# Gated attention unit and token mixer: keys turned as 64 rows, sums over tokens as 64x64 matmuls into one bank

## The chip, the core and the metric

The kernel runs on one core of a Trainium2 chip. The core has a matrix engine (TensorE, PE in the profile, with its weight loads as PEld), three engines for elementwise work (VectorE = DVE, ScalarE = ACT, GpSimd = POOL), a queue that issues DMAs (SyncE = SP) and 16 DMA engines. Matmuls read SBUF and write PSUM, which has eight banks of 2 KB for each of its 128 partitions; DVE and ACT take results out of PSUM, POOL does not read it. The metric is the device time of one execution in microseconds.

## What is computed

Eight sequences (b) of 3200 tokens, 256 wide. The first half is an attention without softmax, the second a token mixer on its result x.

```python
scores = (1.0 / S) * np.matmul(z, z.transpose(0, 2, 1))     # z: 8 x 3200 x 64
attn = np.maximum(scores, 0.0) ** 2
x = u * np.matmul(attn, v)                                   # u, v: 8 x 3200 x 256
wq, wk = x @ w_q, x @ w_k                                    # 256 -> 64
W_tok = (1.0 / 8.0) * np.einsum('bsd,btd->bst', wq, wk)
mixed = np.einsum('bst,btd->bsd', W_tok, x)
out = np.maximum(mixed, 0.0) @ w_out
```

No nonlinearity stands between W_tok and x, so the kernel never forms W_tok: it sums wk^T x over the tokens of a sequence, a 64 x 256 matrix, and multiplies wq by it. This sum over tokens is what the change is about.

## The kernel before

A sequence is cut into 25 tiles of 128 tokens and, for the columns of the attention, into seven groups: six of 512 tokens and a last one of 128 (LASTG). The stages of a sequence:

- Scores (L265). Two tiles of 128 x 512 scores go to one PSUM tile "ps" of two banks. There are two such tiles; scores, projections, mixes and output projections share them, so each new user waits until the one before the last has been read out. DVE or ACT applies ReLU (L291, L287) into g, and POOL or ACT squares it (L309, L307) into a buffer "at", of which there are NAT.
- Turned squares (L331). The attention matrix is symmetric, so blocks near the diagonal are computed once and turned by a DMA on SP into "tt" or "ttl".
- Second product (L352). Squares times v into "acc". Contraction over 128 tokens is split into two matmuls of 64 rows each, which write two banks (r = 0 and 1). A group's output has two halves, so four banks hold it.
- Gate. For each half of a group the two banks are added: one engine copies the first bank to SBUF (L368), DVE adds the second (L369), POOL multiplies by u into x (L388). x is stored so that one DMA (L400) turns it into xT.
- Projections (L417). x times w_q and w_k together, again as two 64-row halves. For half r = 0 of a group wqk holds [q, k] in its 128 columns and for r = 1 [k, q]; so queries of half r lie in partitions r * 64 onward, and keys in the other half of the partitions. Results are copied to "qk" (L430).
- Keys. One DMA (L435) turns all 128 rows of qk, queries included, into "kx", where each token has 64 places of queries and 64 of keys. POOL then writes the keys over the queries (doubling, L447), so that each token has its keys twice.
- Sums over tokens, "heads" in the code (L454). For each 128 tokens, two matmuls of 64 tokens each, with the doubled keys as 128 columns, into two banks: columns 256 to 511 of the PSUM tile whose first columns hold the next group's projections, or a tile of their own ("hd"). DVE adds both banks to "ha" (L469), and at the end of a sequence POOL adds the two halves into "hs" (L476). Because the keys were doubled, hs has the sum in both halves of its partitions, as the mixes need it.
- Mixes (L482) with ReLU out (L503), output projection (L513) with scaling out (L535, L540), store (L541).

The order of instructions on each engine is written out when the program is built. A planner keeps one clock for each engine, adds an assumed duration for each piece of work (give), and puts matmuls one after another; the extras (keys, mixes, projections) become ready at times in those clocks. `lead` sets how far scores run ahead of the second product; a pair p of score tiles may also be made only when the squares of pair p - NAT have been used. `shut` is the time at which the next bank of sums closes, and LATE, SPARE, BIAS shift choices between engines around it. MIXES spaces a sequence's mixes, V0 sets when the first loads of the second sequence's v begin, and KEEP how many tiles a group holds back for its end. DMAs on SP are entered by `move` with their issue time and the time they take on the DMA engines. The last sequence ends by code of its own (from L1082): x^T x for its last three groups ("xtx"), the remaining sum ("hd"), a product with w_k in fp32 ("hl", L565), then mixes and output projections without other work beside them.

Of the kernel before, what the change touches and what calls it, by code (L numbers as in the profile page):

```python
# [16 lines left out]
def kernel(  # L17
# [33 lines left out]

    NAT = 16
    NX = 7
    NXT = 4
    NEARBY = 8
    KEEP = 4

# [239 lines left out]
    def second_stage(p, g, ways):  # L297
        at = pat.tile([P, 2 * W], FP16, tag="at", name="at")
        at0 = 0
        parts = pieces(p)  # L300
        if len(ways) > len(parts):
            parts = [(slice(h, h + 1), parts[0][1]) for h in range(2)]
        for (hs, w), on_act in zip(parts, ways * 2):
            n = hs.stop - hs.start
            out = at[:, at0 : at0 + n * w].rearrange("p (n w) -> p n w", w=w)
            if on_act:
                nc.scalar.square(out=out, in_=g[:, hs, 0:w])  # L307
            else:
                nc.gpsimd.tensor_mul(out=out, in0=g[:, hs, 0:w], in1=g[:, hs, 0:w])  # L309
# [12 lines left out]
        def turn(b, gi, gj, n0, nn, c0, c1):  # L322
            if (b, gi, gj) not in turned:
                if gj == LASTG:
                    tag, nr, bufs = "ttl", 1, 8
                else:
                    homes[b, gi, gj] = home = homes_free.pop(0)
                    tag, nr, bufs = f"tt{home}", 4, 1
                turned[b, gi, gj] = ptt.tile([P, nr, 4, P], FP16, tag=tag, name=tag, bufs=bufs)
            out = turned[b, gi, gj][:].rearrange("p n j t -> p (n j) t")  # L330
            nc.sync.dma_start_transpose(out=out[:, 4 * n0 : 4 * (n0 + nn), :], in_=at[:, c0:c1])  # L331

        return [(x, lambda x=x: turn(*x)) for x in blocks]
# [27 lines left out]

    def gate(b, gi, half):
        if (b, gi) not in xs:
# [48 lines left out]

    def projections(b, gi, ps, stop=True):
        n = min(2, widths[gi] // P)
        for c in range(NC):
            for r in halves(gi):
                nc.tensor.matmul(  # L417
                    out=ps[:, r, 0 : n * P],
                    lhsT=wqk[top(r), c, :, :].rearrange("p t h -> p (t h)"),
                    rhs=xTs[b, gi][top(r), 0:n, c, :],  # L420
                    start=(c == 0),
                    stop=(stop and c == NC - 1),
                )

    def projections_out(b, gi, ps):
# [4 lines left out]
        nc.scalar.copy(out=qks[b, gi][:, 0:nr, 0 : n * P], in_=ps[:, 0:nr, 0 : n * P])  # L430

    def turn_keys(b, gi):
        nn = widths[gi] // P
        ks[b, gi] = pk.tile([P, 4, 2, dh], FP16, tag="kx", name="kx")
        nc.sync.dma_start_transpose(  # L435
            out=ks[b, gi][:, 0:nn, :, :].rearrange("p n a h -> p n (a h)"),
            in_=qks[b, gi][:].rearrange("p r s -> p (r s)")[:, 0 : nn * P],
        )

    doubled = set()  # L440

    def double_keys(b, gi):
        doubled.add((b, gi))
        nn = widths[gi] // P
        for r in halves(gi):
            sl = slice(2 * r, min(2 * r + 2, nn))
            nc.gpsimd.tensor_copy(out=ks[b, gi][:, sl, r, :], in_=ks[b, gi][:, sl, 1 - r, :])  # L447

    def heads(b, gi, ps, begun=()):
        nn = widths[gi] // P  # L450
        assert (b, gi) in doubled
        for n in range(nn):
            for r in range(2):
                nc.tensor.matmul(  # L454
                    out=ps[:, r, D : 2 * D],
                    lhsT=ks[b, gi][top(r), n, :, :].rearrange("p a h -> p (a h)"),
                    rhs=x_rows(b, gi, n)[top(r), :, :],
                    start=(n == 0 and r not in begun),
                    stop=(n == nn - 1),
                )  # L460
        del xs[b, gi]

    def heads_out(b, gi, ps):
        part = ps[:, 0:2, D : 2 * D]
        if gi == 0:
            hacc[b] = psml.tile([P, 2, D], FP32, tag="ha", name="ha")
            nc.vector.tensor_copy(out=hacc[b][:], in_=part)
        else:
            nc.vector.tensor_add(out=hacc[b][:], in0=part, in1=hacc[b][:])  # L469
        if gi == LASTG:  # L470
            heads_done(b)

    def heads_done(b):
        hss[b] = psml.tile([P, D], FP16, tag="hs", name="hs")
        ha = hacc.pop(b)
        nc.gpsimd.tensor_add(out=hss[b][:], in0=ha[:, 0, :], in1=ha[:, 1, :])  # L476

# [11 lines left out]

    def mix_out(b, gi, ps):  # L490
        n = min(2, widths[gi] // P)
# [10 lines left out]
        else:  # L502
            nc.scalar.activation(out=out, in_=ps[:, 0:nr, 0 : ND * n * P], func=RELU)  # L503

# [83 lines left out]
    mixed_at = []  # L588
    MIXES = 18.0
    MIXES_END = 14.0  # L590
# [82 lines left out]
    def squares():  # L673
        while pending and pending[0][0] <= clock[PE] + 0.3:
            ready, p, g = pending.pop(0)
            a, c = max(clock[ACT], ready), max(clock[POOL], ready)
            on_act = a + SPARE < c and (a + 1.06 <= shut() + LATE or a + 2.5 < c)
            ways = [on_act]
            if clock[PE] < UNTIL and max(a + 0.57, c + 0.97) + SPLIT < min(a + 1.06, c + 1.9):
                ways = [a < c, a >= c]  # L680
                done = max(give(ACT, ready, 0.57), give(POOL, ready, 0.97))
            else:
                done = give(ACT, ready, 1.06) if on_act else give(POOL, ready, 1.9)
            for (b, gi, gj, _, nn, _, _), turn in second_stage(p, g, ways):
# [20 lines left out]

    def double(b, gi):
        keys_at[b, gi] = give(POOL, clock[PE], 0.6) + 0.5
        double_keys(b, gi)

    def use_keys(b, gi):  # L710
# [3 lines left out]
        if keyed and keys_at.get(keyed[0], 1e9) <= clock[PE]:  # L714
            prior = keyed.pop(0)
        projections(b, gi, ps, stop=not prior)
        clock[PE] += 0.44 if gi < LASTG else 0.24
        if prior:
            heads(*prior, ps, halves(gi))
            clock[PE] += 0.44 if prior[1] < LASTG else 0.11  # L720
        ready = clock[PE] + FROM_PE
        projections_out(b, gi, ps)
        done = give(ACT, ready, 0.56)
        n = widths[gi] / P
        final = (b, gi) == (last, LASTG - 2)
        if not final:
            move(
                done + SLACK, done + 10.0, 1.28, 0.21 * n, lambda: turn_keys(b, gi),
                lambda t: at_time(t, lambda: double(b, gi)),
            )  # L730
            keyed.append((b, gi))
        if prior:
            heads_out(*prior, ps)
            done = give(DVE, done, 0.7)
            if prior[1] == LASTG:
                give(POOL, done, 0.6)
                heads_known(prior[0])
# [7 lines left out]
    def use_heads():  # L745
# [5 lines left out]
        heads_out(*prior, ps)  # L751
        done = give(DVE, clock[PE] + FROM_PE, 0.7)
        if prior[1] == LASTG:
            give(POOL, done, 0.6)
            heads_known(prior[0])
# [8 lines left out]
    def use_mix(b, gi):  # L764
# [3 lines left out]
        clock[PE] += 0.22  # L768
        mix_out(b, gi, ps)
        done = give(ACT, clock[PE] + FROM_PE, 1.03 if gi < LASTG else 0.3)  # L770
        close_slot(done)
# [40 lines left out]
    ZWAIT, ZDUE, ZSTEP, ZSTEP0 = 14.0, 32.0, 7.0, 5.0  # L812
    V0 = 56
    V1 = 11
# [37 lines left out]

    SPARE = 0.3
    BIAS = 0.2
    XDUE = 5.0
    XWAIT = 7.0
    LATE = 0.3

    def half_done(b, gi, half):
        ready = clock[PE] + FROM_PE  # L860
        t = give(ACT, ready, 0.57)
        t = give(DVE, t, 0.68)
        free_at[half] = t
        if b == last and gi >= LASTG - 2:
            give(DVE, t, 0.75)
        t = give(POOL, t, 1.2)
        gate(b, gi, half)
        if half == halves(gi)[-1]:
# [129 lines left out]
    done_acc = 0  # L998
    lead = 140
    turn_about = False  # L1000
# [40 lines left out]
    while extras or later or moves:  # L1041
        x = next((x for x in extras if x[1] == "proj"), None)
        if not x:
# [4 lines left out]
                or (x[1] == "keys" and len(keyed) < 2)  # L1048
                or keyed[0] in doubled
            ]  # L1050
# [39 lines left out]
    ha = hacc.pop(last)  # L1090
    nc.vector.tensor_add(out=hsum[:], in0=ha[:, 0, :], in1=ha[:, 1, :])
    psl = acc_tile(0, 1, "hl")
# [53 lines left out]
```

## Time and profile before

| | |
|---|---|
| median of 3 runs | 781.1 us (779.43 to 781.89) |
| the profiled execution | 780.0 us from first to last instruction |
| TensorE's granted clock, mean | 0.998 |
| DMA packets | 307116, 141.11 MB |
| DMA queue of SP: share of 16 engines | 85.8% |
| DMA queue of POOL: share of 16 engines | 14.6% |

The profile is of one execution. Busy time of TensorE counts each matmul from its start to a modelled end, so that two matmuls that overlap count once, and a short gap between starts can be covered by a modelled end. In groups of instructions a line reads: source line, engine, operation, tiles written and read, shapes, count, busy time, mean duration of one in ns, and idle time of the engine just before, with what ended it. In the timeline a row begins with its start and its duration, and the idle time before it stands in brackets.

### The profile page before, as it was taken

The page shows a single profiled execution, that of the slowest core. Times are in us where ns is not written, and L with a number is a line of the kernel's source. Part 1 is how long each engine was busy: PE and PEld are TensorE (multiplying, and loading weights), DVE is VectorE, ACT ScalarE, POOL GpSimd, SP SyncE. Part 2 cuts the span into 40 slices and gives each one's busy share as a digit, 9 for nine tenths or more (in the row PEclk, how much of TensorE's full clock was granted, in tenths as well). Part 3 has the DMA queues.
Part 4 walks back from the last instruction along what each step waited for, and adds up shares of the span by engine and source line. Part 5 has one row for each costly group of instructions (what it writes and reads, how often), then busy time and mean ns, then how long its engine had stood idle before and what let it go on. Part 6 is the DMA issues. An engine that isn't in the chain of part 4 may idle for free.

```text
span 780.0 us, 28286 instructions
## 1 busy us (share of the span) xinstructions
PE 765.9 (98%) x12410; PEld 674.0 (86%) x12410; DVE 490.5 (63%) x506; ACT 558.1 (72%) x672; POOL 619.5 (79%) x518
## 2 busy tenths in 40 slices
PE   8999999999999999999999999999999999999996
PEld 6889989988888888988889888898888988999894
DVE  6576768767565766655657556575566765656534
ACT  6786785676877776876678777787778578777644
POOL 7798887668986978887779769887888868887850
PEclk9999999999999999999999999999999999999999
DMA  7899999999999999999899999999989999989725
GB/s 181 157 152 175 162 160 170 171 187 180 222 183 190 200 218 204 151 170 217 198 171 193 168 221 168 199 161 171 241 159 208 162 196 211 157 169 168 183 81 198
DMA packets 307116, 141.11 MB, mean 181 GB/s; under 512 B 285744, under 2 KB 288432, under 8 KB 306992
## 3 DMA queue, kind: packets, MB, share of 16 engines
q1 hardware_dynamic: 300224, 123.13, 85.8%
q0 software_dynamic: 6624, 15.98, 14.6%
q8 instruction: 97, 1.59, 0.9%
q14 instruction: 27, 0.22, 0.1%
q10 hardware_dynamic: 144, 0.20, 0.1%
HBM read 59.64 MB, written 26.21 MB: 110 GB/s over the span
## 4 chain that ended last, share of the span: by engine, by line
PE 94%; DVE 2%; DMA 1%; ACT 1%; issue 1%; POOL 0%; DVEq 0%; SPq 0%
PE acc L352 68%; PE sc L265 13%; PE fo L513 6%; PE qk L417 3%; PE qk L454 2%; PE mx L482 1%; DVE g L291 1%; DMA v_sb<-in_v_dram 1%; ACT g L287 1%; DVE both L369 0%; DVE fo L535 0%; DMA z<-in_z_dram 0%; ACT at L307 0%; PE xtx L555 0%; PE hd L454 0%
## 5 line engine op out<-in xcount | busy, mean ns | idle before, releaser
L352 PE MATMUL acc<-v_sb,at 64*128 64x256 f16 x7344 | 506.0, 269 | 2.3 <-issue 1.5
L309 POOL TENSOR_TENSOR at<-g 128x1024 f16<-128x1024 f32 (+2 forms) x240 | 432.5, 1813 | 88.0 <-DVE g L291 46.8
L352 PEld LDWEIGHTS <-at 64*128 64x128 f16 x7344 | 403.9, 94 | 54.5 <-issue 9.7
L291 DVE TENSOR_SCALAR g<-sc 128x1024 f32<-128x1024 f32 (+2 forms) x302 | 349.9, 1175 | 121.8 <-PE sc L265 109.8
L307 ACT ACTIVATE at<-g 128x1024 f16<-128x1024 f32 (+2 forms) x242 | 241.6, 1015 | 25.0 <-DVE g L291 22.5
L287 ACT ACTIVATE g<-sc 128x1024 f32<-128x1024 f32 (+2 forms) x177 | 174.8, 990 | 56.2 <-PE sc L265 50.9
L265 PE MATMUL sc<-zT 64*128 64x512 f16 x924 | 185.3, 375 | 2.4 <-DVE g L291 1.2
L388 POOL TENSOR_TENSOR x_sb<-both,u_sb 128x512 f16<-128x512 f32 (+1 forms) x112 | 134.3, 1205 | 48.9 <-DVE both L369 48.4
L352 PE MATMUL acc<-v_sb,tt 64*128 64x256 f16 x2272 | 168.0, 269 | 0.0
L352 PEld LDWEIGHTS <-tt 64*128 64x128 f16 x2272 | 127.0, 94 | 10.3 <-issue 0.6
L369 DVE TENSOR_TENSOR both<-acc,both 128x512 f32<-128x512 f32 (+1 forms) x104 | 69.5, 670 | 70.9 <-ACT both L368 62.0
L368 ACT COPY both<-acc 128x512 f32<-128x512 f32 (+1 forms) x104 | 58.9, 566 | 66.5 <-PE acc L352 63.1
L265 PEld LDWEIGHTS <-zT 64*128 64x128 f16 x924 | 62.2, 94 | 9.8 <-issue 5.2
L535 DVE TENSOR_SCALAR fo<-fo 128x1024 f32<-128x1024 f32 (+2 forms) x31 | 32.7, 1067 | 41.4 <-PE fo L513 41.3
L503 ACT ACTIVATE rt<-mx 128x1024 f16<-128x1024 f32 (+1 forms) x49 | 45.5, 931 | 12.2 <-PE mx L482 12.0
L430 ACT CAST qk<-qk 128x512 f16<-128x512 f32 (+1 forms) x54 | 29.4, 544 | 29.2 <-PE qk L454 25.4
L513 PE MATMUL fo<-wo,rt 128*128 128x256 f16 x400 | 49.4, 273 | 0.1
L469 DVE TENSOR_TENSOR ha<-qk,ha 128x512 f32<-128x512 f32 x37 | 25.6, 691 | 36.1 <-ACT qk L430 35.8
L513 PEld LDWEIGHTS <-rt 128*128 128x128 f16 x400 | 36.4, 98 | 10.8 <-issue 6.5
L540 ACT ACTIVATE fo<-fo 128x1024 f32<-128x1024 f32 (+2 forms) x27 | 24.6, 914 | 19.8 <-PE fo L513 19.8
L417 PE MATMUL qk<-xT_sb,wqk 64*128 64x256 f16 (+1 forms) x404 | 32.2, 265 | 0.0
L454 PE MATMUL qk<-x_sb,kx 64*128 64x256 f16 x360 | 29.1, 269 | 0.0
(44 smaller groups left out, 237.0 us busy)
## 6 DMA issues: line engine op xcount, KB each, us to landing
u_sb<-in_u_dram SPq DMA_DIRECT2D x48, 512.0 KB, 5.0
out_dram<-fo SPq DMA_DIRECT2D x46, 512.0 KB, 4.4
v_sb<-in_v_dram POOLq DMA_DIRECT2D x35, 320.0 KB, 6.2
zn<-in_z_dram POOLq DMA_DIRECT2D x7, 400.0 KB, 6.3
tt<-at SPq DMA_TRANSPOSE x143, 4.5
u_sb<-in_u_dram SPq DMA_DIRECT2D x8, 128.0 KB, 3.6
out_dram<-fo SPq DMA_DIRECT2D x8, 128.0 KB, 3.5
out_dram<-fo SPq DMA_DIRECT2D x4, 256.0 KB, 4.2
```

Source lines behind the costliest of these rows:

```text
L265: nc.tensor.matmul(out=sc[:, h, 0:gw], lhsT=z_cols(b, h, ti * P, P), rhs=z_cols(b, h, gs, gw), start=True, stop=True,)
L287: nc.scalar.activation(out=g[:, hs, 0:w], in_=sc[:, hs, 0:w], func=RELU, scale=GSCALE)
L291: nc.vector.tensor_scalar(out=g[:, hs, 0:w], in0=sc[:, hs, 0:w], scalar1=0.0, scalar2=GSCALE, op0=AOP.max, op1=AOP.mult,)
L307: nc.scalar.square(out=out, in_=g[:, hs, 0:w])
L309: nc.gpsimd.tensor_mul(out=out, in0=g[:, hs, 0:w], in1=g[:, hs, 0:w])
L352: nc.tensor.matmul(out=accs[half, r][:, ds((j % 2) * D, D)], lhsT=weights(b, gi, ti, j)[top(r), :], rhs=vs[b][top(r), ti, :], start=(first ...
L368: nc.scalar.copy(out=both[:, 0 : n * D], in_=accs[half, 0][:, 0 : n * D])
L369: nc.vector.tensor_add(out=both[:, 0 : n * D], in0=accs[half, 1][:, 0 : n * D], in1=both[:, 0 : n * D])
L388: nc.gpsimd.tensor_mul(out=xs[b, gi][:, 0:n, :, r, :].rearrange("p n c d -> p (n c) d"), in0=both[:, 0 : n * D].rearrange("p (m d) -> p m ...
L417: nc.tensor.matmul(out=ps[:, r, 0 : n * P], lhsT=wqk[top(r), c, :, :].rearrange("p t h -> p (t h)"), rhs=xTs[b, gi][top(r), 0:n, c, :], st ...
L503: nc.scalar.activation(out=out, in_=ps[:, 0:nr, 0 : ND * n * P], func=RELU)
L513: nc.tensor.matmul(out=banks[r][:, ds(j * D, D)], lhsT=flat[:, ds((dc * n + j) * P, P)], rhs=wo[:, dc, :], start=(dc == 0 and j == 0), sto ...
```

## The change

- The DMA that turned qk as a whole becomes two for each group (one for the last, narrow group). Each turns only the 64 partitions that hold keys, of one half r. kx now has 64 places for each token.
- The doubling on POOL is gone, with the planner's step for it.
- The sums over tokens use the 64 key columns. The matmul of the tokens in rows r * 64 onward writes partitions r * 64 onward, both into the same bank. ha has half the columns.
- ha's two halves now lie on different partitions. `sum_halves` copies each half to the other's partitions (POOL; in the last sequence DVE) and adds.
- NAT goes from 16 to 18, KEEP from 4 to 6, lead from 140 to 200; MIXES, V0, SPARE, BIAS and LATE change too.
- The planner may put the first copy of the gate, the copy of qk and the ReLU of the mixes on DVE as well as on ACT, and squares on DVE (which it never does in the built program). Some assumed durations change.

```diff
-    NAT = 16
+    NAT = 18
...
-    KEEP = 4
+    KEEP = 6
...
-    def gate(b, gi, half):
+    def gate(b, gi, half, by_act):
...
-        nc.scalar.copy(out=both[:, 0 : n * D], in_=accs[half, 0][:, 0 : n * D])
+        copy = nc.scalar.copy if by_act else nc.vector.tensor_copy
+        copy(out=both[:, 0 : n * D], in_=accs[half, 0][:, 0 : n * D])
...
     def turn_keys(b, gi):
+        n = min(2, widths[gi] // P)
+        ks[b, gi] = pk.tile([P, 4, dh], FP16, tag="kx", name="kx")
+        for r in halves(gi):
+            nc.sync.dma_start_transpose(
+                out=ks[b, gi][:, 2 * r : 2 * r + n, :],
+                in_=qks[b, gi][top(1 - r), r, 0 : n * P],
+            )
...
-    def double_keys(b, gi):
-        doubled.add((b, gi))
-        nn = widths[gi] // P
-        for r in halves(gi):
-            sl = slice(2 * r, min(2 * r + 2, nn))
-            nc.gpsimd.tensor_copy(out=ks[b, gi][:, sl, r, :], in_=ks[b, gi][:, sl, 1 - r, :])
...
         for n in range(nn):
             for r in range(2):
                 nc.tensor.matmul(
-                    out=ps[:, r, D : 2 * D],
-                    lhsT=ks[b, gi][top(r), n, :, :].rearrange("p a h -> p (a h)"),
+                    out=ps[top(r), 0, D : 2 * D],
+                    lhsT=ks[b, gi][top(r), n, :],
                     rhs=x_rows(b, gi, n)[top(r), :, :],
-                    start=(n == 0 and r not in begun),
+                    start=(n == 0),
                     stop=(n == nn - 1),
                 )
...
+            hss[b] = psml.tile([P, D], FP16, tag="hs", name="hs")
+            sum_halves(hacc.pop(b), hss[b], nc.gpsimd.tensor_copy, nc.gpsimd.tensor_add)
+
+    def sum_halves(ha, out, copy, add):
+        crossed = psum.tile([P, 2 * D], FP32, tag="both", name="hx")
+        for r in range(2):
+            copy(out=crossed[top(r), 0:D], in_=ha[top(1 - r), :])
+        add(out=out[:], in0=ha[:], in1=crossed[:, 0:D])
...
-    MIXES = 18.0
+    MIXES = 10.0
...
-    V0 = 56
+    V0 = 48
...
-    SPARE = 0.3
-    BIAS = 0.2
+    SPARE = 0.1
+    MORE = 3.0
+    BIAS = -0.3
...
-    LATE = 0.3
+    LATE = 0.1
...
-    lead = 140
+    lead = 200
...
-    nc.vector.tensor_add(out=hsum[:], in0=ha[:, 0, :], in1=ha[:, 1, :])
+    sum_halves(ha, hsum, nc.vector.tensor_copy, nc.vector.tensor_add)
```

More of the change, by code (lines that the diff above doesn't have):

```diff
@@ L715, in use_keys @@
             prior = keyed.pop(0)
-        projections(b, gi, ps, stop=not prior)
+        projections(b, gi, ps)
         clock[PE] += 0.44 if gi < LASTG else 0.24
         if prior:
-            heads(*prior, ps, halves(gi))
+            heads(*prior, ps)
             clock[PE] += 0.44 if prior[1] < LASTG else 0.11
         ready = clock[PE] + FROM_PE
-        projections_out(b, gi, ps)
-        done = give(ACT, ready, 0.56)
+        a, d = (max(clock[x], ready) for x in (ACT, DVE))
+        by_act = a + 0.58 <= d + 0.69 or d + 0.69 > shut() + LATE + 0.6
+        projections_out(b, gi, ps, by_act)
+        done = give(ACT, ready, 0.58) if by_act else give(DVE, ready, 0.69)
         n = widths[gi] / P
@@ L768, in use_mix @@
         clock[PE] += 0.22
-        mix_out(b, gi, ps)
-        done = give(ACT, clock[PE] + FROM_PE, 1.03 if gi < LASTG else 0.3)
+        ready = clock[PE] + FROM_PE
+        a, d = (max(clock[x], ready) for x in (ACT, DVE))
+        by_act = a + 1.03 <= d + 1.22 or d + 1.22 > shut() + LATE + 0.6
+        mix_out(b, gi, ps, by_act)
+        if by_act:
+            done = give(ACT, ready, 1.03 if gi < LASTG else 0.38)
+        else:
+            done = give(DVE, ready, 1.22 if gi < LASTG else 0.42)
         close_slot(done)
```

77 lines of the change are left out of this document (36 added, 41 removed).

## The prediction

> **What bounds the kernel now.** I read the page first, then TensorE's busy time by stretches, its groups by shape, the chain of waits, and the timeline around the places where TensorE changes what it does.
>
> ```profile
> span 780.0 us, 28286 instructions
> PE 765.9 (98%) x12410; PEld 674.0 (86%) x12410; DVE 490.5 (63%) x506; ACT 558.1 (72%) x672; POOL 619.5 (79%) x518
> PE 94%; DVE 2%; DMA 1%; ACT 1%; issue 1%; POOL 0%; DVEq 0%; SPq 0%
> 0.00:20.00 20.00, 16.17 (x200) 12.53 (x202) 13.49 (x18) 12.76 (x21) 15.49 (x23) 1.00 0.77 183
> 20.00:40.00 20.00, 19.24 (x316) 16.86 (x314) 11.72 (x13) 13.89 (x20) 13.66 (x11) 1.00 0.90 160
> 40.00:60.00 20.00, 19.69 (x319) 17.95 (x318) 15.37 (x15) 17.64 (x20) 19.28 (x15) 1.00 1.03 147
> 100.00:120.00 20.00, 18.51 (x313) 17.22 (x311) 13.13 (x14) 15.34 (x17) 16.20 (x15) 1.00 1.30 167
> 120.00:400.00 280.00, 279.88 (x4620) 244.43 (x4616) 180.81 (x184) 200.07 (x237) 224.78 (x187) 1.00 1.07 188
> 400.00:420.00 20.00, 19.47 (x300) 16.81 (x297) 12.53 (x12) 15.56 (x18) 15.88 (x16) 1.00 1.08 190
> 420.00:760.00 340.00, 339.93 (x5573) 300.55 (x5567) 205.81 (x211) 246.88 (x292) 278.05 (x224) 1.00 0.98 179
> 760.00:780.00 20.00, 13.05 (x122) 8.70 (x118) 9.74 (x14) 8.55 (x18) 1.65 (x2) 0.94 0.52 198
> ```
>
> The second number of a stretch is its length, the third TensorE's busy time. TensorE is the bound from the first to the last 20 us: the chain of waits is 94% TensorE, and between 20 and 760 us the visible idle time is 0.76 + 0.31 + 1.49 + 0.12 + 0.53 + 0.07 = 3.3 us (60 to 100 us has none). The 1.49 us among it is one wait that the timeline gives to "issue", to nothing that the profile shows. So freed time on the other engines, and better covered waits, can bring about 3 us; whatever lengthens the stream of matmuls is paid in full. Both sides of this change must therefore be looked for on TensorE.
>
> The pace of that stream:
>
> ```profile
> L454 PE MATMUL qk<-x_sb,kx 64*128 64x256 f16 x360 | 29.1, 269 | 0.0
> L454 PE MATMUL hd<-x_sb,kx 64*128 64x256 f16 x22 | 3.0, 270 | 0.0
> L513 PE MATMUL fo<-wo,rt 128*128 128x256 f16 x400 | 49.4, 273 | 0.1
> 355.50 2.18 PE acc L352 x40
> ```
>
> "64*128" is the part of the array that an instruction takes, rows by columns, and the next term its operand. Forty matmuls of the second product take 2.18 us: two at a time, one on each half of the rows, so 0.109 us a pair though one alone is shown as 269 ns.
>
> **The sums over tokens: new shape on TensorE.** They are 360 + 22 = 382 matmuls, 191 pairs, before and after. Now each multiplies by 64 columns instead of 128 and writes its own half of the partitions; 256 columns still stream through, so a pair keeps 0.109 us and nothing is gained. Weight loads stay hidden: 94 ns for 128 columns against 109 ns, and 64 columns have half as many.
>
> But the shape of the array's part changes from 64*128 to 64*64. What happens where a shape changes and where it doesn't:
>
> ```profile
> 231.06 0.71 PE L352 MATMUL acc<-v_sb,tt 64*128 64x256 f16 x10
> 231.61 0.60 PE L417 MATMUL qk<-xT_sb,wqk 64*128 64x256 f16 x8
> 232.04 0.60 PE L454 MATMUL qk<-x_sb,kx 64*128 64x256 f16 x8
> 232.48 0.38 PE L352 MATMUL acc<-v_sb,tt 64*128 64x256 f16 x4
> 220.79 0.64 PE L352 MATMUL acc<-v_sb,tt 64*128 64x256 f16 x7
> 221.35 1.64 PEld L513 LDWEIGHTS <-rt 128*128 128x128 f16 x16 [0.21 <-issue]
> 221.36 1.92 PE L513 MATMUL fo<-wo,rt 128*128 128x256 f16 x16
> 223.21 0.22 PEld L352 LDWEIGHTS <-at 64*128 64x128 f16 x6 [0.21 <-issue]
> 223.21 0.39 PE L352 MATMUL acc<-v_sb,at 64*128 64x256 f16 x4
> ```
>
> At 232 us the sums over tokens stand between projections and second product, all 64*128: eight matmuls start 0.44 us after the eight before, no gap. At 221 us the output projection is 128*128, and both on the way in and on the way out the weight load stands idle for 0.21 us and starts only with its matmul. The last matmul before it starts at 220.79 + 0.64 - 0.269 = 221.16 and the next at 221.36: 0.20 us instead of 0.109, so a change of shape costs 0.09 us. On the way out it is 221.36 + 1.92 - 0.273 = 223.01 to 223.21, again 0.09. No row has 64*64, so the price of a change to it lies between 0 (as between lines 417, 454 and 352, which change only what is multiplied) and 0.093 us (as around line 513). I take 0.093, since the shape does change, and every change of shape looked at here pays it.
>
> The Trainium skill states this: in "TensorEngine Tiling (Array Packing)", under Tiling Modes, Key Properties, "Changing tiling mode (not just tile) drains the TensorE". The rows at 221 and 223 us agree for 128*128; no row here shows it for 64*64. It gives no price; by the rule the upper end holds, without it the lower one.
>
> In the order in which the changed program's instructions stand on TensorE, the sums enter 64*64 53 times, 45 of them behind projections inside one bank group, and leave it 53 times; the only 128*128 neighbours are in the tail. Against before these are 104 more changes of shape (two of the 106 were paid already), and the output projections save two. 104 x 0.093 - 2 x 0.093 = +9.5 us, with 0 as the other end.
>
> **Keys, doubling, queues.** 53 transposes of 128 rows become 99 of 64 rows on SP, and 99 copies leave POOL.
>
> ```profile
> L435 SPq DMA_TRANSPOSE kx<-qk x53: 1121/1287/3884, 54.1 to 740.9; - x53
> DMA to landing us min/median/max: 2.3/4.9/8.2
> L447 POOL COPY kx<-kx 128x128 f16<-128x128 f16 x92 | 24.5, 298 | 0.0
> L430 ACT CAST qk<-qk 128x512 f16<-128x512 f32 x47 | 27.5, 585 | 25.4 <-PE qk L454 21.7 <-PE qk L417 3.3
> SPq L331 <- POOL at L309: 51.1, 35, 3.2
> SPq L331 <- ACT g L287: 38.7, 18, 8.1
> ```
>
> SP issues 46 more, 46 x 1.29 = 59 us of its time, if a half-size transpose takes as long to issue as a whole one (the far bound; half of it the near one). SP spends more than that waiting for data (51.1 + 38.7 us in these two rows alone). Queued behind each pair are the transposed squares (L331), the x blocks and the stores. A key block now is needed at the earliest 13.4 us of TensorE work after its projection (14.9 before); copy 0.59, two issues 2.6 and landing 4.9, at worst 8.2, make 8.1 to 11.4 us. So this is hidden, at no cost, by second-product work; were the cover gone, the sums would wait up to 2 us a block. Half the key bytes leave the DMA queues, and 24.5 us leave POOL: both worth nothing by themselves, as no wait of TensorE ends there.
>
> **End of a batch.** The halves of the sum must now cross partitions: two POOL copies of 64x256 and an add instead of one add.
>
> ```profile
> L207 POOL CAST wqk<-w32s 64x256 f16<-64x256 f32 x4 | 1.5, 397 | 0.1
> 238.02 0.72 POOL L476 TENSOR_TENSOR hs<-ha 128x256 f16<-128x256 f32 x1
> 239.35 0.38 PE L482 MATMUL mx<-qk,hs 64*128 64x256 f16 x4
> L469 DVE TENSOR_TENSOR ha<-qk,ha 128x512 f32<-128x512 f32 x37 | 25.6, 691 | 36.1 <-ACT qk L430 35.8
> ```
>
> 2 x 0.40 more on POOL, and the add on DVE falls from 0.69 to the 0.42 of a 128x256 one: +0.53 us from the last sum to the mix. At 238 us, among the tightest, the sum was ready 239.35 - 238.74 = 0.6 us early, and the mixes' distance behind the last sum stays at 3.9 to 6.2 us of TensorE work (4.0 to 4.9 before). Hidden by 0.1 us at worst; without it up to 0.5 us seven times.
>
> In the last batch there is no cover:
>
> ```profile
> 762.16 0.42 DVE L1086 COPY G<-xtx 128x256 f32<-128x256 f32 x1 [0.62 <-PE xtx L555]
> 762.71 1.13 PE L565 MATMUL hl<-G,wk 128*128 128x256 f32 x4
> 762.82 0.69 DVE L469 TENSOR_TENSOR ha<-hd,ha 128x512 f32<-128x512 f32 x1 [0.23 <-PE hd L454]
> 763.55 0.42 DVE L1091 TENSOR_TENSOR hm<-ha 128x256 f32<-128x256 f32 x1
> 764.08 0.42 DVE L1098 TENSOR_TENSOR hs<-hl,hm 128x256 f16<-128x256 f32 x1
> 764.56 0.39 PE L482 MATMUL mx<-qk,hs 64*128 64x256 f16 x4 [0.18 <-DVE hs L1098]
> ```
>
> DVE: 0.69 + 0.42 become 0.42 + 2 x 0.42 + 0.42, +0.57 us, and line 1098 and the mix wait for it. At best the copies are shorter and hl (ending 763.84) still sets the start: 0. I take +0.5.
>
> **The replanned order.** More squares ahead (18 buffers, lead 200), copies of sums shifted to DVE (65 of 104) and first evictions to ACT: by counts and the rows' durations DVE and POOL each lose about 20 us, ACT gains about 7, and none gets near TensorE's 98%. In the new order a square is used at least 4.4 us behind its scores outside the first 25 us (3.2 before; median 12.4 instead of 8.1), and a bank of sums is reopened no earlier than 1.8 us after closing (1.36). That speaks for most of the 3.3 us above, without the "issue" wait: -1.8 us, between -3.3 and +1 for new collisions. The first 22 us of TensorE's work stand in the old order.
>
> **Sum.** 780.0 + 9.5 + 0.5 - 1.8 = 788.2 us in the profiled execution's terms. That execution lies 1.1 us under the median of the runs (781.1; 779.43 to 781.89), so about 789 us.
>
> **Rivals.** (1) 64*64 costs nothing: for it speaks that rows 231 to 232 change tile without a gap, against it the rows at 221 and 223. Then 781.1 + 0.5 - 1.8 - 0.2 (two changes saved) = 779.6, and with the whole 3.3 us gone 778.1: say 778.5, on the other side; it decides from a price under 0.01 us a change. (2) The two matmuls of a pair write one bank and go one after the other: 191 x 0.109 = +20.8 us on top, 810. For it: before, the halves always had banks of their own (ps[:, r]); against it: they now have partitions of their own. The Trainium skill's "TensorEngine Tiling (Array Packing)", Restrictions and Gotchas, Gotcha 1, says that different row tiles cannot access one bank at once; no run here shows it. (3) Shapes cost nothing but the replanning misses: keys or the crossed sum come late by 0.5 us in the 53 groups' thinner cover in, say, 10 places, +5: 784. Against it the covers above.
>
> **How the numbers follow.** Forecast 0.56, (1) 0.32, (2) 0.04, (3) 0.08. The runs of before spread over 0.3%, so less than that is no change: under 778.8 is faster, over 783.4 slower. Of (1) I count 0.23 faster and 0.09 the same, of (3) 0.06 slower and 0.02 the same; with the forecast and (2) slower has 0.66, same 0.11, faster 0.23. The forecast's own range is 786 (0.065 us a change) to 792 (no gain from the order). The range reaches down to (1): 777 to 792.
>
> **What would show it.** Right: weight loads of kx with 0.2 us idle put to "issue", likewise the first load behind them, the sums' matmuls shown as 64*64 and still in pairs; TensorE's busy time longer by some 8 us, since modelled ends cover part of each gap. Wrong: projections, sums and second product following each other at 0.109 us a pair, as at 232 us (rival 1), or sums starting one by one every 0.109 us (rival 2). Rival 3 would show as waits of TensorE for DMA kx or POOL hs. The last mix behind hs should start about 0.5 us later than now, counted from the end of xtx.

## The result, and the profile after

| | before | after |
|---|---|---|
| median of 4 runs | 781.0 us (779.43 to 781.89) | 792.1 us (790.6 to 794.2) |
| ratio after to before, 95% interval | | 1.0139 (1.0112 to 1.0165) |
| the profiled execution, first to last instruction | 780.0 us | 788.8 us |
| TensorE's granted clock, mean | 0.998 | 0.998 |

The change makes the kernel 11.1 us slower. A run's time lies 1.7 to 1.9 us above its span wherever a run shows both (790.6 to 788.8 here; only e3_two_banks has 2.1 to 2.2), so the profiled execution of before, with 780.0 us, was one of its longer ones (about 781.8) and that of after its shortest: the spans differ by 8.8 us only. The ratios below leave out runs that were disturbed, so they aren't always the quotient of the medians.

The page of after, in the rows that answer to those of before: span, busy times, and the chain of waits by engine.

```profile
span 788.8 us, 28214 instructions
PE 774.2 (98%) x12410; PEld 633.0 (80%) x12410; DVE 470.4 (60%) x532; ACT 562.8 (71%) x647; POOL 601.4 (76%) x433
PE 92%; DVE 2%; POOL 2%; issue 1%; DMA 1%; ACT 1%; DVEq 0%; POOLq 0%
```

The same 12410 matmuls keep TensorE busy 8.3 us longer (765.9 before), while DVE lost 20 us and POOL 18 us without any effect. By stretches (the second number is the length, the third TensorE's busy time):

```profile
20.00:40.00 20.00, 19.71 (x328) 17.68 (x324) 13.78 (x15) 16.44 (x21) 16.05 (x12) 1.00 0.98 160
...
120.00:400.00 280.00, 279.55 (x4528) 227.35 (x4524) 169.31 (x189) 205.89 (x229) 220.92 (x156) 1.00 1.00 179
...
420.00:760.00 340.00, 338.09 (x5466) 274.01 (x5464) 196.60 (x219) 243.82 (x277) 258.88 (x178) 1.00 0.95 175
760.00:780.00 20.00, 19.10 (x238) 14.49 (x233) 11.41 (x20) 9.88 (x19) 5.19 (x4) 1.00 0.33 115
780.00:790.00 10.00, 2.04 (x18) 1.32 (x16) 2.87 (x4) 1.43 (x3) 0.00 (x0) 0.82 0.62 247
```

Between 120 and 400 us only 4528 matmuls start instead of 4620, in a stretch as full as before: the stream is slower, not interrupted. Visible idle time between 20 and 760 us is 0.29 + 0.45 + 1.91 = 2.65 us (40 to 120 and 400 to 420 us have none), against 3.3 us before. What lengthens the stream stands in the groups of waits of TensorE and its weight loads (total us, times, longest) and in TensorE's rows of the timeline around one group of sums:

```profile
PEld L353 <- issue: 12.8, 59, 0.7
PEld L449 <- issue: 9.2, 43, 0.3
PEld L514 <- issue: 6.5, 31, 0.2
...
PEld L449 <- DMA kx<-qk: 2.2, 1, 2.2
PE hd L449 <- DMA kx<-qk: 1.9, 1, 1.9
```

```profile
232.94 0.60 PE L419 MATMUL qk<-xT_sb,wqk 64*128 64x256 f16 x8
233.47 0.35 PEld L449 LDWEIGHTS <-kx 64*64 64x64 f16 x8 [0.21 <-issue]
233.47 0.62 PE L449 MATMUL qk<-x_sb,kx 64*64 64x256 f16 x8
234.02 0.44 PEld L353 LDWEIGHTS <-tt 64*128 64x128 f16 x10 [0.20 <-DMA out_dram<-fo]
234.02 0.72 PE L353 MATMUL acc<-v_sb,tt 64*128 64x256 f16 x10
```

The weight load of the keys stands idle for 0.21 us on the way in, as the output projection's did before (31 times, 6.5 us, in both kernels), and the second product's does on the way out; the name of a DMA beside it there is the last event the profile found, not a load that these matmuls need. From the first projection to the first matmul of the second product pass 234.02 - 232.94 = 1.08 us; the same 16 matmuls took 232.48 - 231.61 = 0.87 us before. Over all such stretches between 20 and 760 us (eight projections, eight sums, and then the second product or scores), worked out from the starts of the matmuls in the traces, the median is 0.873 us before (37 stretches) and 1.087 us after (35), the mean 0.876 and 1.106. Two changes of shape thus cost 0.21 to 0.23 us, one 0.107 to 0.115. The same starts show where that time lies. From the last projection to the first sum pass 0.199 us instead of 0.105, from the last sum to the next stage 0.202 instead of 0.105, and the second pair of sums starts 0.134 us behind the first instead of 0.109; the other pairs keep 0.109 us (medians). The idle time of a weight load, 0.2 us at each change, is therefore about twice what the stream loses there.

Not all is that. One block of keys was late, by 1.9 us, as the rows of SP's DMAs (SPq), of that copy and of the sums in the timeline of after show:

```profile
598.58 0.29 DVE L433 CAST qk<-qk 128x128 f16<-128x128 f32 x1
...
599.57 8.00 SPq L332 DMA_TRANSPOSE tt<-at  x2
607.66 3.13 SPq L439 DMA_TRANSPOSE kx<-qk  x2
...
612.24 1.18 SPq L439 DMA_TRANSPOSE kx<-qk  x1
...
617.55 0.30 PE L449 MATMUL hd<-x_sb,kx 64*64 64x256 f16 x2 [1.91 <-DMA kx<-qk]
```

What SP itself waited for between 597 and 618 us, in its groups of waits:

```profile
SPq L332 <- ACT at L307: 3.6, 2, 3.2
SPq L332 <- POOL at L310: 2.3, 1, 2.3
```

The keys of a last, narrow group were copied by 598.87 us. Their transpose stood in SP's queue behind transposes of squares (8.0 us for two, since SP waited 3.2 and 2.3 us for squares that weren't made yet; the rest of the 3.6 us belongs to a third) and behind the two of the group before; it was issued at 612.24, and its data were there 5.3 us later. The matmuls had 617.55 - 1.91 - 598.87 = 16.8 us of cover, and it was not enough. The place in the queue alone doesn't make a block late: e3_two_banks below has the same order, and there the same block was copied by 601.58 us and issued 12.2 us later, but landed after 2.3 us instead of 5.3, by 616.05 us and so 2.2 us before its matmuls:

```profile
613.78 1.18 SPq L439 DMA_TRANSPOSE kx<-qk  x1
...
618.29 0.30 PE L449 MATMUL hd<-x_sb,kx 64*64 64x256 f16 x2
```

The end of the last batch, from x^T x to the first mix, in the same timeline:

```profile
768.36 2.13 PE L556 MATMUL xtx<-xd 128*128 128x256 f16 x18
...
771.09 0.42 DVE L464 TENSOR_TENSOR ha<-hd,ha 128x256 f32<-128x256 f32 x1 [0.24 <-PE hd L449]
771.62 0.59 DVE L472 COPY hx<-ha 64x256 f32<-64x256 f32 x2
772.24 0.42 DVE L473 TENSOR_TENSOR hm<-ha,hx 128x256 f32<-128x256 f32 x1
772.77 0.42 DVE L1108 TENSOR_TENSOR hs<-hl,hm 128x256 f16<-128x256 f32 x1
773.25 0.61 PE L479 MATMUL mx<-qk,hs 64*128 64x256 f16 x8 [0.60 <-DVE hs L1108]
```

From the start of xtx to the mix it takes 4.89 us; before it was 764.56 - 760.10 = 4.46 us, so the crossed sum costs 0.43 us there.

### The profile page after: what moved, and what is told of

Its sections match the earlier page's. It is cut to its first block, busy times and chain, and to the rows that moved or that the text cites. A ratio compares the mean times of both kernels' runs of the same rounds, so it can differ in the third digit from the quotient of the medians.

```text
span 788.8 us, 28214 instructions
## 1 busy us (share of the span) xinstructions
PE 774.2 (98%) x12410; PEld 633.0 (80%) x12410; DVE 470.4 (60%) x532; ACT 562.8 (71%) x647; POOL 601.4 (76%) x433
## 4 chain that ended last, share of the span: by engine, by line
PE 92%; DVE 2%; POOL 2%; issue 1%; DMA 1%; ACT 1%; DVEq 0%; POOLq 0%
PE acc L353 66%; PE sc L265 12%; PE fo L514 6%; PE qk L449 3%; PE qk L419 3%; PE mx L479 1%; POOL at L310 1%; DVE g L291 1%; DMA kx<-qk 1%; POOL x_sb L390 0%; DMA z<-in_z_dram 0%; DVE fo L536 0%; ACT g L287 0%; DVE zd L122 0%; PE hd L449 0%
## 5 line engine op out<-in xcount | busy, mean ns | idle before, releaser
L353 PEld LDWEIGHTS <-at 64*128 64x128 f16 x7344 | 366.7, 94 | 81.8 <-issue 11.0
L291 DVE TENSOR_SCALAR g<-sc 128x1024 f32<-128x1024 f32 (+1 forms) x247 | 291.0, 1192 | 149.0 <-PE sc L265 140.3
L287 ACT ACTIVATE g<-sc 128x1024 f32<-128x1024 f32 (+1 forms) x231 | 222.8, 977 | 94.2 <-PE sc L265 87.2
L307 ACT ACTIVATE at<-g 128x1024 f16<-128x1024 f32 (+1 forms) x242 | 240.0, 1015 | 9.7 <-DVE g L291 7.7
L353 PE MATMUL acc<-v_sb,tt 64*128 64x256 f16 x2272 | 148.9, 269 | 0.0
L370 DVE COPY both<-acc 128x512 f32<-128x512 f32 (+1 forms) x65 | 43.8, 673 | 64.7 <-PE acc L353 64.3
L265 PEld LDWEIGHTS <-zT 64*128 64x128 f16 x924 | 51.5, 94 | 11.1 <-issue 5.5
L541 ACT ACTIVATE fo<-fo 128x1024 f32<-128x1024 f32 (+2 forms) x46 | 41.4, 943 | 20.5 <-PE fo L514 20.5
L370 ACT COPY both<-acc 128x512 f32<-128x512 f32 (+1 forms) x39 | 22.0, 563 | 41.2 <-PE acc L353 39.8
L502 ACT ACTIVATE rt<-mx 128x1024 f16<-128x1024 f32 (+1 forms) x30 | 26.6, 894 | 10.1 <-PE mx L479 9.9
L504 DVE TENSOR_SCALAR rt<-mx 128x1024 f16<-128x1024 f32 (+1 forms) x19 | 22.2, 1180 | 13.8 <-PE mx L479 13.8
```

Of the source, the lines that this page charges most:

```text
L265: nc.tensor.matmul(out=sc[:, h, 0:gw], lhsT=z_cols(b, h, ti * P, P), rhs=z_cols(b, h, gs, gw), start=True, stop=True,)
L287: nc.scalar.activation(out=g[:, hs, 0:w], in_=sc[:, hs, 0:w], func=RELU, scale=GSCALE)
L291: nc.vector.tensor_scalar(out=g[:, hs, 0:w], in0=sc[:, hs, 0:w], scalar1=0.0, scalar2=GSCALE, op0=AOP.max, op1=AOP.mult,)
L353: nc.tensor.matmul(out=accs[half, r][:, ds((j % 2) * D, D)], lhsT=weights(b, gi, ti, j)[top(r), :], rhs=vs[b][top(r), ti, :], start=(first ...
L541: nc.scalar.mul(out=flat_out[:, sl], in_=part, mul=FINAL_SCALE)
```

## The experiments

The first four separate the shape of the sums from everything else. All ratios are to the kernel before.

**The new sums alone, in the old order** (e1_sums_alone). Before, with its whole transposes, doubling and planner; only the sums and the end of a batch are new.

```diff
-                    out=ps[:, r, D : 2 * D],
-                    lhsT=ks[b, gi][top(r), n, :, :].rearrange("p a h -> p (a h)"),
+                    out=ps[top(r), 0, D : 2 * D],
+                    lhsT=ks[b, gi][top(r), n, 0, :],
...
+            sum_halves(hacc.pop(b), hss[b], nc.gpsimd.tensor_copy, nc.gpsimd.tensor_add)
```

> The kernel before with only the sums over tokens changed: 64 key columns taken from the doubled keys, both halves into one bank, halves crossed at the end of a sequence. Transposes of keys, doubling, plan and order stay. Changes of shape on TensorE: 176 instead of 72. Theory (a change of shape between 64*128 and 64*64 costs about 0.10 us): 104 x 0.10 = 10.4, and 0.5 in the tail, so about 792 us (789 to 795). Rival (the shape costs nothing, the replanned order and the keys' transposes cost the 11 us): 781 to 782.

Measured: 791.9 us (791.71 to 792.02), ratio 1.0153 (1.0136 to 1.0169), so +11.9 us over the 780.0 us of before beside it: the whole loss, and somewhat more, without the changed DMAs, planner and constants. Its trace has 176 changes of shape where before has 72, and its timeline the same gaps:

```profile
232.91 0.60 PE L417 MATMUL qk<-xT_sb,wqk 64*128 64x256 f16 x8
233.44 0.36 PEld L454 LDWEIGHTS <-kx 64*64 64x64 f16 x8 [0.21 <-issue]
233.44 0.62 PE L454 MATMUL qk<-x_sb,kx 64*64 64x256 f16 x8
234.00 0.22 PEld L352 LDWEIGHTS <-tt 64*128 64x128 f16 x6 [0.20 <-issue]
234.00 0.50 PE L352 MATMUL acc<-v_sb,tt 64*128 64x256 f16 x6
```

104 more changes at 0.107 to 0.115 us are 11.1 to 12.0 us, and the end of the last batch adds about 0.4.

**Two banks** (e3_two_banks). After, but the two matmuls of a pair write banks of their own, and DVE adds them with two instructions.

```diff
-                    out=ps[top(r), 0, D : 2 * D],
+                    out=ps[top(r), r, D : 2 * D],
...
+        for r in range(2):
+            part, ha = ps[top(r), r, D : 2 * D], hacc[b][top(r), :]
```

> The changed kernel, with each half of a sum in a bank of its own again (64*64 as before, 174 changes of shape as in the changed kernel; DVE reads the two halves in two instructions). Theory (the shape change costs, the common bank doesn't): as the changed kernel, 791 to 793, pairs starting together as there. Rival (the common bank holds the second matmul of a pair up, or is what makes the switch slow): 4 us or more below the changed kernel.

Measured: 793.7 us (791.95 to 796.61), ratio 1.0180 (1.0156 to 1.0204). The stretch of projections and sums lasts as long as in after (median 1.091 us, 1.087 there). So the common bank costs nothing: a pair on different partitions of one bank goes at full pace. The weight loads of the next scores now wait a little for the second instruction on DVE:

```profile
PEld L265 <- DVE ha L466: 2.4, 10, 0.2
```

The Trainium skill, in "TensorEngine Tiling (Array Packing)", Restrictions and Gotchas, Gotcha 1, says that different row tiles cannot access the same PSUM bank at once. These 64*64 tiles, which differ in rows and in columns, do so at 0.109 us a pair; here the measurement decides.

**Sums in two visits** (e4_sums_in_two_visits). After, but each group's sums are cut in two, between the halves of the projections: the same matmuls with 262 changes of shape instead of 174.

```diff
+            if c % 2 and between:
+                between.pop(0)()
...
+        between = [lambda ns=ns: heads(*prior, ps, ns) for ns in ((0, 1), (2, 3))] if prior else []
+        projections(b, gi, ps, between, bool(prior) and prior[1] < LASTG)
```

> The changed kernel with every sum that follows projections in a bank split in two visits, after the second and after the fourth quarter of the projections: the same matmuls, 262 changes of shape instead of 174. Theory: 88 x 0.10 = +9 us on the changed kernel, about 801 (798 to 804). Rival (64*64 matmuls are slow in themselves, or something else in the change costs the time): within 2 us of the changed kernel.

Measured: 800.6 us (798.1 to 802.7), ratio 1.0263 (1.0232 to 1.0294): 8.5 us more than after for 88 more changes, 0.096 us each (by the spans, 796.3 - 788.8 = 7.5 us, 0.085; each against the before measured beside it, 780.0 and 781.0 us, 20.5 - 11.1 = 9.4 us, 0.107). Its timeline shows what a change costs when nothing else differs:

```profile
235.23 0.38 PE L419 MATMUL qk<-xT_sb,wqk 64*128 64x256 f16 x4
235.54 0.14 PEld L451 LDWEIGHTS <-kx 64*64 64x64 f16 x4 [0.21 <-issue]
235.54 0.41 PE L451 MATMUL qk<-x_sb,kx 64*64 64x256 f16 x4
...
235.88 0.39 PE L419 MATMUL qk<-xT_sb,wqk 64*128 64x256 f16 x4
...
236.20 0.41 PE L451 MATMUL qk<-x_sb,kx 64*64 64x256 f16 x4
...
236.54 0.72 PE L353 MATMUL acc<-v_sb,tt 64*128 64x256 f16 x10
```

Four changes: 236.54 - 235.23 = 1.31 us instead of eight pairs' 0.87, so 0.11 us each.

**The old shape with the new keys** (e5_wide_keys). After, but each sum takes 128 columns again, the 64 places in front of the keys and the keys; the first 64 columns' results are not used. Two banks, two additions on DVE, 70 changes of shape.

```diff
-                    out=ps[top(r), 0, D : 2 * D],
-                    lhsT=ks[b, gi][top(r), n, :],
+                    out=ps[:, r, D : 2 * D],
+                    lhsT=ks[b, gi][top(r), n : n + 2, :].rearrange("p a h -> p (a h)"),
```

> The changed kernel with 128 columns again, but without doubling: beside a token's 64 keys the 64 places before them are loaded as well, whose products land in partitions that nobody reads; each half in a bank of its own, DVE adds both into the upper partitions (one more instruction a group), two copies spread the sum. Turned keys, plan and order as in the changed kernel; 70 changes of shape. Theory: the changed kernel less 104 x 0.10, about 781.5 (779 to 784). Rival (the plan or the transposes cost it): 788 or more. Where it ends against 781 tells what the rest of the change brings.

Measured: 786.6 us (785.6 to 788.82), ratio 1.0089 (1.0071 to 1.0107): 5.5 us less than after (4.5 us, each against the before measured beside it), by useless columns. Neither forecast holds. The second addition probably took back a part, since the planner still counted 0.43 us for both and weight loads waited for it:

```profile
PEld L265 <- DVE ha L472: 5.9, 17, 0.5
PEld L419 <- DVE ha L472: 1.8, 5, 0.4
```

**The same with the additions planned** (e6_wide_keys_planned: the planner counts 0.87 us for them) **and with one addition** (e6b_wide_keys_one_add: one DVE instruction over both banks, 17 square buffers).

```diff
-            done = give(DVE, done, 0.43)
+            done = give(DVE, done, 0.87)
```

> The kernel with 128 columns, turned keys and no doubling once more, with its order made anew: the planner is told the 0.87 us that DVE's two instructions for a sum take, instead of 0.43. In the run before scores and projections stood still for DVE's additions to ha 22 times, 7.7 us by the weight loads. Theory (that was all that held it above the kernel before): 780 to 782. Rival (the turned keys or the plan cost time even without the shape): 784 or more.

> As the last one, with the sum's two banks added by one DVE instruction (ha has room for both again, so 17 buffers of squares instead of 18), planned at 0.70 us. Theory: 780 to 782, like the last. Rival: 784 or more.

Measured: 783.9 us (779.33 to 797.0), ratio 1.0031 (1.0012 to 1.0050), and 784.8 us (783.73 to 792.96), ratio 1.0082 (1.0049 to 1.0115). The waits for additions to ha are gone from both, which speaks for that reading, though the order is a new one too. The first lies between its two forecasts, the second in its rival's range. The first is the nearest to before of all kernels with the new keys, and no version beat before. In the second, TensorE waited 3.3 us for two key blocks.

Six kernels then asked what the rest of the change is worth.

**The new plan alone** (e7_plan_alone). After's planner and constants with the old keys, doubling and sums, and 16 square buffers, as memory asks.

> Keys, doubling and sums as in the kernel before; the changed kernel's planner and all its constants but one (16 buffers of squares, since the old tiles leave no room for 18). 72 changes of shape. Theory as forecast (the order brings about 1.8 us): 778 to 780. Rival (the order brings nothing, or collides): 780 to 784.

Measured: 781.6 us (780.86 to 783.72), ratio 1.0020 (1.0010 to 1.0030): 1.1 us slower than before beside it (780.5), no gain.

**The new keys alone** (e8_keys_alone). Before's planner and constants, two DMAs of 64 rows a group, no doubling, 128-column sums as in e5_wide_keys, but with one addition. The order is made anew by the same planner.

```diff
+            nc.sync.dma_start_transpose(
+                out=ks[b, gi][:, 2 * r + 1 : 2 * r + 1 + n, :],
+                in_=qks[b, gi][top(1 - r), r, 0 : n * P],
+            )
```

> The kernel before with its own plan's constants, keys turned as 64 rows by two DMAs, no doubling, 128 columns with the places before a token's keys as idle half, halves in two banks. Theory (turned keys and freed POOL are worth nothing where TensorE is the bound): 779 to 781.5, no change. Rival (46 more issues on SP make blocks late): 782 or more, with TensorE waiting for DMAs.

Measured: 786.6 us (784.35 to 792.43), ratio 1.0094 (1.0065 to 1.0123). This looked like a price of 6 us for the second DMA of each group, since one wait of TensorE for keys, 1.8 us, stands among many small ones.

**After with whole transposes** (e9_shape_whole_turns): one DMA a group, doubling, the 64*64 sums of after, 17 square buffers. **Before without doubling** (e10_before_no_doubling): one whole transpose, 128 columns taken across neighbouring tokens so that keys stand in the upper half, lower half unused. **The same under after's planner** (e11_plan_no_doubling), with 16 square buffers.

```diff
-                    lhsT=ks[b, gi][top(r), n, :, :].rearrange("p a h -> p (a h)"),
+                    lhsT=ks[b, gi][top(r), :, :, :].rearrange("p n a h -> p (n a h)")[:, (2 * n - n // 2) * dh : (2 * n - n // 2 + 2) * dh],
```

> The changed kernel with its keys turned whole again (one DMA of 128 rows a group, doubling on POOL) but the 64*64 sums into one bank kept; 17 buffers of squares, since the larger key tiles leave no room for 18. Theory (with the drains in it the stream of matmuls leaves enough room that the second DMA costs nothing more): 791 to 793, with runs closer together than the changed kernel's 790.6 to 794.2. Rival (the second DMA a group costs 4 us or more here too, as it seems to under 128 columns): 786 to 789.

> The kernel before without doubling, otherwise with its keys turned whole: the 128 columns loaded for a token are a window whose upper half is its keys; what the lower half gives lands in partitions that nobody reads. It differs from the run keys_alone (786.6) in one DMA a group instead of two and in the order made anew. Theory (the second DMA a group is what cost 6 us there): 779.5 to 781.5. Rival (the lost doubling copies or the new reads cost it): 784 or more.

> The same sums and whole turns under the changed kernel's planner and constants, 16 buffers of squares. Theory (the new order is worth nothing, POOL's freed 24 us neither): 780 to 782. Rival (the new order pays once its keys come by one DMA and POOL is free): 778 or less.

Measured: 789.2 us (788.48 to 789.58), ratio 1.0095 (1.0072 to 1.0118); 786.7 us (785.82 to 788.88), ratio 1.0074 (1.0047 to 1.0101); 782.6 us (781.57 to 788.82), ratio 1.0031 (1.0009 to 1.0052). e9_shape_whole_turns lies between its two forecasts, beside the rival's. It is 7.6 us above e7_plan_alone, which differs in the sums, their additions and one square buffer, and 3 us below after.

That 7.6 us is less than the shape's 11 to 12 us has to do with idle time: between 20 and 760 us TensorE stands visibly idle for 5.0 us in e7_plan_alone and for 1.5 us in e9_shape_whole_turns. TensorE's busy time, which leaves idle time out, differs by 10.8 us (764.9 and 775.7). It parts all the kernels here by the shape of their sums: 763.7 to 768.9 us in the eight with 64*128 (before among them), 774.2 to 777.7 us in the five with 64*64, and 784.4 us in e4_sums_in_two_visits. Of the 3 us to after, the spans show 788.8 - 787.4 = 1.4 us, no more than the one late block of 1.9 us.

e10_before_no_doubling takes the theory of the second DMA away: with one DMA it is as slow as e8_keys_alone. Nor do the missing doubling or the new reads slow it by themselves, since e11_plan_no_doubling has both and is 4 us faster. What those two kernels share is an order made anew under the old constants. In e10_before_no_doubling the span is 4.1 us above that of before; visible idle time between 20 and 760 us makes up 1.7 us of it (5.0 instead of 3.3) and busy time 1.9 us (767.8 instead of 765.9). Its weight loads of the second product and the scores wait 14.7 us in 43 places and 7.7 us in 21 for "issue" (before 10.5 in 35 and 5.2 in 15), for which the profile names no cause. A late block doesn't need the second DMA either: e11_plan_no_doubling has one DMA a group, and its matmuls waited 1.4 us for a block.

**After with one whole transpose** (e12_shape_one_turn): as e9_shape_whole_turns, without the doubling.

```diff
-                    lhsT=ks[b, gi][top(r), n, :],
+                    lhsT=ks[b, gi][top(r), n, 1 - n // 2, :],
```

> The changed kernel with one part undone: qk is turned whole by one DMA a group again (kx has the queries beside the keys), the sums over tokens read the 64 key columns from it as 64x64 matmuls into one bank, still without doubling; 17 square buffers, and the planner counts the keys as ready 0.5 us behind their transpose instead of 0.3. It stands between the changed kernel (792.1) and e9_shape_whole_turns (789.2), which had the doubling as well. Theory, that the second DMA of a group cost the some 3 us between those two: 788 to 790, with no wait of TensorE for DMA kx over 1 us. Rival, that e9 was only the luckier order, since any new order of this kernel lies some us up or down: 791 to 794, whatever the number of DMAs, and the waits over 0.3 us between 20 and 760 us sum to more than e9's.

Measured: 793.4 us (793.33 to 794.71), ratio 1.0181 (1.0167 to 1.0195). With one DMA a group, and no wait of TensorE for keys in its list of waits, it is no faster than after, as the rival said. But it pays in another place, which the rows of POOL, of the last addition and of the mix show in its timeline:

```profile
430.51 3.75 POOL L310 TENSOR_TENSOR at<-g 128x1024 f16<-128x1024 f32 x2
431.55 0.41 DVE L463 TENSOR_TENSOR ha<-hd,ha 128x256 f32<-128x256 f32 x1
434.21 1.26 POOL L390 TENSOR_TENSOR x_sb<-both,u_sb 128x512 f16<-128x512 f32 x1
435.42 0.59 POOL L152 DMA_DIRECT2D v_sb<-in_v_dram  x1
436.06 0.82 POOL L471 COPY hx<-ha 64x256 f32<-64x256 f32 x2
436.97 0.71 POOL L472 TENSOR_TENSOR hs<-ha,hx 128x256 f16<-128x256 f32 x1
437.74 0.39 PE L478 MATMUL mx<-qk,hs 64*128 64x256 f16 x4 [2.97 <-POOL hs L472]
```

The last sum was ready at 431.96 us, but POOL had two squares, a gate and a DMA to issue first, so the copies began 4.1 us later and the mix waited 3.0 us. Three such waits of the matmuls sum to 3.6 us in this execution; in after there is one, of 0.2 us. Without them the time would be about 789.8 us (793.4 - 3.6), inside the theory's range, so this run doesn't settle the price of the second DMA.

## Why the prediction was right, and where its terms were off

**The bound and the sign: right.** The stream of matmuls was paid in full, and 20 us less on DVE and 18 us less on POOL brought nothing. e1_sums_alone shows that the new sums alone make the loss, e3_two_banks that it isn't the common bank, and e4_sums_in_two_visits that it grows with the number of changes. The median of 792.1 us lies at the very top of the forecast's own range, 786 to 792.

**The price of a change of shape: right in kind, too small.** Forecast 0.093 us, from the output projections; measured 0.107 to 0.115 us, by the stretches of projections and sums. For 104 changes that is 11.1 to 12.0 us instead of 9.7. The gap itself was forecast well (0.199 - 0.105 = 0.094 on the way in, 0.202 - 0.105 = 0.097 on the way out); what the forecast left out is the second pair of each visit, 0.025 us late. The Trainium skill, in "TensorEngine Tiling (Array Packing)", Tiling Modes, Key Properties, says that a change of tiling mode drains TensorE. The rows agree for 64*64 in that both changes leave a gap; that the gap is a drain they don't show. TensorE's busy time grew by 8.3 us where some 8 were foreseen, but by 10.6 in e1_sums_alone with as many changes, so this close a match is chance. Rival 1 (no price) is excluded by these rows.

**One bank: right.** Rival 2 asked for 20.8 us more; e3_two_banks and the pace of after show no price at all.

**Keys hidden at no cost: wrong once in the profiled execution.** The step that failed is the sum "copy 0.59, two issues 2.6 and landing 4.9, at worst 8.2": it began at the copy and left out that SP's queue makes the transposes wait behind those of squares whose data aren't ready, 13.4 us in the rows above (copied at 598.87, issued at 612.24). Together with a landing of 5.3 us that cost 1.9 us once, rival 3 at one place. The forecast that the smaller transpose takes as long to issue as a whole one (the far bound, 59 us of SP) came true, and for a quarter of the size, since 64 x 256 elements took the place of 128 x 512:

```profile
L439 SPq DMA_TRANSPOSE kx<-qk x99: 1114/1228/2435, 62.5 to 752.8; - x99
DMA to landing us min/median/max: 2.3/3.6/8.9
```

The median issue is 1.23 us (for whole ones 1.29 in before, 1.22 in e9_shape_whole_turns). Whether the second DMA has a price beyond that single wait is not shown: e9_shape_whole_turns, with one DMA, was 3 us faster than after by the medians (1.4 by the spans), and e12_shape_one_turn, with one DMA as well, was not.

**End of a batch: right.** Forecast +0.5 us in the last batch, measured +0.43. In the batches before, the crossed sum was hidden in after as assumed, but for one mix that waited 0.2 us. But the price "without it up to 0.5 us seven times" was too low: e12_shape_one_turn paid 3.0 us at one place, because the copies stand behind squares on POOL.

**The replanned order: its gain was given back.** Forecast -1.8 us. The "issue" wait of 1.5 us at 116 us is gone, and the visible idle time fell from 3.3 to 2.65 us; without the late keys it would have fallen to about 0.7 (2.65 - 1.9). But e1_sums_alone, in the old order, hasn't that wait either (TensorE is busy for all of 100 to 120 us) and has 1.9 us of visible idle time in all, so the wait probably belonged to the one execution that was profiled, and there was less to gain than 3.3 us. By the medians nothing is left of it: after (+11.1 us) and e1_sums_alone in the old order (+11.9) are equal within their intervals, and e7_plan_alone shows no gain with the old sums (+1.1).

**The sum.** Forecast 9.5 + 0.5 - 1.8 = +8.2 us in the profiled execution's terms, where +8.8 came out, so 788.8 for 788.2. That they come so close is luck: a long execution of before (about 781.8 us, median 781.0) is compared with the shortest of after (790.6, median 792.1), which hides 2.3 us. The step from 788.2 to "about 789" also set a span beside times of runs; by the medians the forecast is 781.0 + 8.2 = 789.2 us, 2.9 us too low. By the medians it is +11.1, with 11.1 to 12.0 for the shape, 0.4 for the end, -0.2 for two changes saved, and -0.2 to -1.1 us for all the rest. The two longest runs of after (793.43 and 794.2 us) have no trace; what they pay beyond the profiled one is open.

**What stays open.** Orders of the same work by the same planner differ by some us: 779.8, 780.8, 784.1 and 785.2 us of span in e7, e11, e10 and e8, all with 64*128 sums. In the last two more weight loads wait for what the profile calls "issue"; what causes that was not found, and their excess isn't fully accounted for.

## What to carry to other kernels

In a kernel whose matmul stream is the bound, count how often the order of instructions changes the shape of the array's part, and charge about 0.1 us for each (0.085 to 0.115 here, by the ways of counting above); the old shape with half of its columns wasted was 4.5 to 5.5 us cheaper here than the exact one. When a small copy or a transpose is counted as hidden, add what stands in front of it on its queue (13.4 us on SP, 4.1 us on POOL in these traces), not only its own duration. A term of 1 or 2 us for a better order is worth no more than the spread between orders, which was about 5 us here.

## What was not expected of the hardware

```profile
L449 PEld LDWEIGHTS <-kx x382: 102/106/108, 79.6 to 770.7; 64*64 64x64 f16 x191
L449 PE MATMUL hd<-x_sb,kx x28: 269/293/294, 139.5 to 770.8; 64*64 64x256 f16 x28
```

Loading 64 columns into a 64*64 part is shown with 106 ns, and 128 columns into a 64*128 part with 94 ns: half the columns load no faster, though the prediction argued from half as many (hidden in both). The first matmuls behind a change are shown with 293 ns instead of 269, and there the second pair starts 0.134 us behind the first instead of 0.109.
